# Attention and MLP block: maxima from 128 keys, weighted sums in bursts of three and four key tiles, exponentials over two PSUM banks

## The chip, the cores and the metric

The kernel runs on one core of a Trainium2 chip. The metric is the device time of one execution in microseconds. The kernel works on five engines with a queue each: PE (matmuls, with weight loads PEld), ACT (activation functions), DVE (vector operations), POOL and SP (which issues most DMAs). PE writes its results to PSUM, which has 8 banks of 128 partitions x 512 float32 values; ACT and DVE read them there.

## The reference

One transformer block over 2048 tokens of width 448, all in float32: attention with 16 query heads that share one head of keys and values (width 28), and an MLP of width 1792, both on the normalised input, added to it.

```python
xn = _layernorm(x)                      # S, D, H = 2048, 448, 16; Dh = 28
q = (xn @ wq).reshape(B, S, H, Dh)      # 16 heads of queries
k = xn @ wk                             # one head of keys and of values
v = xn @ wv
scores = einsum("bhqd,bkd->bhqk", q, k) * (Dh ** -0.5)
p = softmax(scores)
A = einsum("bhqk,bkd->bhqd", p, v) ... @ wo
h = gelu(layernorm(xn) @ w1 + b1)       # F = 1792
out = x + A + h @ w2 + b2
```

## The kernel before, in words

The first 360 us hold the projections of queries, keys and values and the MLP. Queries go to DRAM (`qd`), the MLP's result rows too (`ad`). The change lies in the rest, the attention, and in the last MLP slots that prepare it.

**Units.** Attention has `NU` = 16 units: 4 chunks of 512 queries times 4 groups of 4 heads. A unit has 16 key tiles (`kt`) of 128 keys. For each key tile and head j, PE makes a score tile of 128 keys x 512 queries (`score`, line 617, output `m`), ACT takes its exponential into `p` in SBUF (line 618), and PE multiplies it by the values into `po` (`pv`, line 791). The weighted sum of a head has 32 output columns, so four heads stand side by side in one PSUM bank; each float32 weighted sum is two matmuls in the profile, so that a key tile has 8 rows of line 791.

**Order.** Nothing reorders the instructions (`manual_schedule`): the order of the code is the order in each engine's queue. A step is two key tiles, written by `ORDERS`: `s` is a score with its exponential, `m` one job of the next unit's maxima, `n` one step of the unit's normalisation, `o` one tile of the output projection, `e` the end of the maxima, and `P` the weighted sums of `BURST` = 2 key tiles, one step behind the scores.

**PSUM in attention.** Seven single banks (`ring`, taken by `mtile` and `score`) turn around among scores, maxima and projection tiles; one bank (`op`) holds `po`. A bank is taken again when the engine that reads it has ended.

**Maxima.** The exponential needs a number per query and head near the greatest score. `max_jobs(u + 1)`, from key tile 6 of unit u on, multiplies each 128 queries by the first 256 keys (`km`, `HEAD` = 256): 16 matmuls of 256 columns in 8 jobs, each followed by one DVE reduction over a PSUM bank (line 491) into `mr`, queries on partitions. `load_max` then has PE transpose `mr` (line 472), two DVE operations negate it and split it in a high and a low part, and two DMAs write these as rows 60 and 124 of the unit's query tile `qs`, so that the score matmul subtracts them. `load_q(u)` loads a unit's queries by four DMAs; for unit 1 it is called when attention's loop begins.

**Normalisation and projection.** `norm_jobs` copies `po`, divides by the sums and splits the result (`oth`, `otl`). After the fourth unit of a chunk, `o_jobs` makes four projection tiles of 12 matmuls each (lines 686 to 688) and DVE adds them to rows loaded from `ad` (line 690). For the last chunk the parts of its first three units, nine matmuls a tile, are made within the last five steps, and those of the last unit after it, in `end_jobs`, where PE first runs idle transposes (`spin`, line 389) while DVE works.

If a sum of squares is too great, a branch (`redo`) computes attention anew with full maxima; it isn't taken here.

Of the kernel before, what the change touches and what calls it, by code (L numbers as in the profile page):

```python
# [15 lines left out]
P = 128  # L16
# [18 lines left out]
HD = D // 2  # L35
# [3 lines left out]
def block_kernel(ctx, tc, x, wq, wk, wv, wo, w1, b1, w2, b2, out):  # L39
# [4 lines left out]
    def f(t):  # L44
        return t.bitcast(F32)
# [61 lines left out]
    def mtile(shape):  # L107
        return mp.tile(shape, F32, name="m")
# [278 lines left out]
    def spin(n, t=None):  # L387
        for _ in range(n):
            pe.matmul(idle if t is None else t, ident, ident, start=True, stop=True)
# [80 lines left out]
    def spread_max(mr, qs):  # L470
        pm = mtile([4 * CT, P])
        pe.transpose(pm, mr, ident)
        mn = keep.tile([4 * CT, 2, P], F32R, name="mn", bufs=1)
        dve.tensor_scalar(mn[:, 0, :], pm, -1.0, 0.0, op0=ALU.mult, op1=ALU.add)
        dve.scalar_tensor_tensor(mn[:, 1, :], pm, -1.0, f(mn[:, 0, :]), op0=ALU.mult, op1=ALU.subtract)
        nc.sync.dma_start(f(qs[60:61, :, :]), f(mn[:, 0, :]))
        nc.sync.dma_start(f(qs[124:125, :, :]), f(mn[:, 1, :]))

    def load_max(u):
        while mxs.step():  # L480
            pass
        spread_max(mrs.pop(u), qss[u])

    def max_jobs(u):
        mrs[u] = keep.tile([P, 4 * CT], F32, name="mr", bufs=2)
        for j in range(4):
            for t in range(0, CT, 2):
                pm = mtile([P, 2, HEAD])
                for k in range(2):
                    pe.matmul(pm[:, k], qss[u][:, j, (t + k) * P:(t + k + 1) * P], km, start=True, stop=True)  # L490
                dve.tensor_reduce(mrs[u][:, CT * j + t:CT * j + t + 2], pm, axis=AX.X, op=ALU.max)  # L491
                yield

    class Stream:
        def __init__(self):
# [131 lines left out]
    for n in range(len(mslots) + LAG):  # L627
        c, ft = mslots[n] if n < len(mslots) else (NCH, n - len(mslots))
        if 3 <= ft < 11 and ft % 2 and c < NCH - 1:
            line(CT * (c + 1) + (ft - 3) // 2)  # L630
        if 9 < ft:
            line(CT * c + ft - 10)
            if ft > 10:
                a = lines[CT * c + ft - 11]
                dve.tensor_add(a, a, b2b)
        if ft == 0 and n:
            a = lines[CT * c - 1]
            dve.tensor_add(a, a, b2b)
        if (c, ft) == (NCH - 1, 7):
            load_q(0)  # L640
        if (c, ft) == (NCH - 1, 9):
            mxs.add(max_jobs(0))
        if (c, ft) == (NCH - 1, 11):
            load_max(0)
        for done, _ in enumerate(slot(n)):
            if done % 5 == 4 and (c, ft) in ((NCH - 1, 9), (NCH - 1, 10)):
# [32 lines left out]
    def o_jobs(c, gs, tiles=range(CT)):  # L679
        last = NG - 1 in gs  # L680
        for k in tiles:
            po = mtile([P, D])
            ts = slice(k * P, (k + 1) * P)
            for g in gs:
                oth, otl = ots[c, g]
                pe.matmul(po, oth[:, ts], woh[:, g, :], start=(g == gs[0]), stop=False)  # L686
                pe.matmul(po, oth[:, ts], wol[:, g, :], start=False, stop=False)  # L687
                pe.matmul(po, otl[:, ts], woh[:, g, :], start=False, stop=(g == gs[-1]))  # L688
            a = rows[c, k]
            dve.tensor_add(a, a, po)  # L690
            if last:
                (nc.scalar if k % 2 and c == NCH - 1 else nc.sync).dma_start(ov[:, CT * c + k, :], a)
            yield

    def o_tiles(c, g):
# [41 lines left out]
    def end_jobs(u, po, halves_of):  # L737
        while side.step() or oside.step():
            pass
        c, g = units[u]  # L740
        oth, otl = o_tiles(c, g)
        jobs = o_jobs(c, [g])
        tr, rb, on = att.tile([P, CW], F32, name="tr2", bufs=1), att.tile([P, CW], F32, name="tr", bufs=1), att.tile([P, CW], F32, name="oc", bufs=1)
        rc = att.tile([P, CW // 32], F32, name="rc", bufs=1)
        last = mtile([P, P])
        halves_of(1)
        sq = att.tile([P, CW], F32, name="sq", bufs=1)
        act.activation(sq, po, AF.Square, accum_out=seen[:, u:u + 1])
        spin(6, last)

        def blocks(t, h):
            return t[:, h].rearrange("p (a b) -> p a b", b=32)

        def shares(i):
            h, r = slice(256 * i, 256 * i + 256), slice(8 * i, 8 * i + 8)
            dve.transpose(tr[:, h], po[:, h])
            dve.reciprocal(rc[:, r], blocks(tr, h)[:, :, 0])
            dve.transpose(blocks(rb, h), rc[:, r, None].to_broadcast([P, 8, 32]))
            dve.tensor_mul(on[:, h], po[:, h], rb[:, h])
            act.activation(oth[:, h], on[:, h], AF.Copy)  # L760
            return lambda: dve.tensor_sub(otl[:, h], on[:, h], f(oth[:, h]))

        low = shares(0)
        low()
        low = shares(1)
        next(jobs)
        low()
        judge()
        for _ in jobs:
            pass  # L770

    pos = {}

# [12 lines left out]
    def pv(u, kt):  # L786
        if kt == 0:
            pos[u] = op.tile([P, CW], F32, name="po")
        po = pos[u]
        for j in range(4):  # L790
            pe.matmul(po[32 * j:32 * j + 32, :], vs[:, kt, :], ps.pop((u, kt, j)),  # L791
                      start=(kt == 0), stop=(kt == NT - 1))
        if kt == NT - 1:
            side.add(norm_jobs(u, pos.pop(u)))
            side.step()
            c, g = units[u]
            if c < NCH - 1 and g == NG - 1:
                oside.add(o_wait(c, range(NG), range(CT)))

    def o_wait(c, gs, tiles):  # L800
        for k in range(4):
            load_rows_of(c, tiles[k:k + 1])
            yield
            yield
        yield from o_jobs(c, gs, tiles)

    steps = [(u, kt) for u in range(NU) for kt in range(0, NT, 2)]
    pvq = [(u, kt) for u in range(NU) for kt in range(NT)]
    for n, (u, kt) in enumerate(steps):
        if n == len(steps) - 14:  # L810
            load_rows_of(NCH - 1, range(CT))
        if 4 <= n < 4 + NG:
            prep_wo(n - 4)
        if u + 1 < NU and kt == 0:
            load_q(u + 1)
        if u + 1 < NU and kt == 6:
            mxs.add(max_jobs(u + 1))
        jobs = [(u, kt + k, j) for k in range(2) for j in range(4)] if n else []
        for what in ORDERS[n % 2]:
            if what == "s" and jobs:  # L820
                score(*jobs.pop(0))
            elif what == "m":
                mxs.step()
            elif what == "e":
                if kt == 12 and u + 1 < NU:
                    load_max(u + 1)
            elif what == "n":
                side.step()
            elif what == "o":
                if n == len(steps) - 5:  # L830
                    oside.add(o_jobs(NCH - 1, range(NG - 1)))
                oside.step()
            elif what == "P":
                assert not jobs
                for _ in range(BURST if n else 0):
                    pv(*pvq.pop(0))
    assert pvq and all(u == NU - 1 for u, kt in pvq)
    pv_last(NU - 1, [kt for u, kt in pvq])
    while side.step():
        pass  # L840
    while oside.step():
# [24 lines left out]
    def general():  # L866
        for u in range(NU):
# [25 lines left out]
            dve.tensor_sub(otl, oc, f(oth))  # L893
            if g == NG - 1:
                load_rows_of(c, range(CT))
                for _ in o_jobs(c, range(NG)):
# [27 lines left out]
```

## Time and profile before

| | |
|---|---|
| median of 3 runs | 942.48 us (942.17 to 944.52) |
| the profiled execution | 944.04 us, its span 942.1 us |
| busy, share of the span | PE 98%, ACT 76%, DVE 44%, POOL 6% |
| chain that ended last | PE 90%, DVE 4%, DMA 3% |
| granted TensorE clock, mean | 0.994 |

A profile's span is the time from the first to the last instruction of one execution; its rows name the line, engine, operation, output and inputs, shape and count. In a row of groups stand busy time, mean ns of one, and the engine's idle time before them with who ended it. In a row of the timeline stand start, length, engine, line and count, and in brackets the idle time before. Matmuls overlap, so that the start of one to the start of the next is what one costs, not its length. A row of busy time by stretch has PE, PEld, DVE, ACT, POOL, then the granted clock, the DMA share and GB/s.

### The profile page before, as it was taken

How to read it: one execution, taken by the hardware profiler on the slowest of the kernel's cores; microseconds unless marked ns; L12 is line 12 of the kernel's file. 1: busy time of each engine (PE TensorE's matmuls, PEld its weight loads, DVE VectorE, ACT ScalarE, POOL GpSimd, SP SyncE). 2: the span in 40 equal slices, each digit the busy share in tenths (PEclk: the TensorE clock that was granted, in tenths of full speed). 3: DMA queues.
4: the chain of work that ended last, by engine and by line, in shares of the span. 5: the costliest groups of instructions: out<-in, count | busy, mean ns of one | idle time of the engine just before them, and what ended most of it. 6: DMA issues, size and time to landing. Idle time of an engine off the chain costs nothing.

```text
span 942.1 us, 13663 instructions
## 1 busy us (share of the span) xinstructions
PE 922.4 (98%) x5261; PEld 606.8 (64%) x5261; DVE 418.2 (44%) x812; ACT 716.2 (76%) x1366; POOL 61.1 (6%) x69
## 2 busy tenths in 40 slices
PE   9999999999999997999999999999999999999996
PEld 8778888888888875545455565455564455564554
DVE  6778776666676661233224233224232223232213
ACT  5787664554645446999999879999869999969973
POOL 4340000000000004000000000000000000000000
PEclk9999999999999999999999999999999999999999
DMA  9772212002004004101102201102201102202001
GB/s 279 223 232 79 71 47 88 21 10 88 21 10 98 0 22 113 41 1 40 41 9 52 70 31 40 41 2 59 70 31 40 41 2 59 70 30 80 1 1 42
DMA packets 34218, 54.07 MB, mean 57 GB/s; under 512 B 5207, under 2 KB 22805, under 8 KB 34149
## 3 DMA queue, kind: packets, MB, share of 16 engines
q1 hardware_dynamic: 32740, 52.58, 19.5%
q8 instruction: 42, 0.69, 0.3%
q10 hardware_dynamic: 1408, 0.57, 0.2%
q14 instruction: 28, 0.22, 0.1%
HBM read 37.40 MB, written 14.68 MB: 55 GB/s over the span
## 4 chain that ended last, share of the span: by engine, by line
PE 90%; DVE 4%; DMA 3%; ACT 1%; issue 1%; POOL 0%; SPq 0%; DVEq 0%; ACTq 0%
PE m L617 26%; PE po L791 25%; PE ph L171 12%; PE m L560 5%; PE m L557 5%; PE m L563 5%; PE m L490 4%; PE m L687 1%; PE m L686 1%; PE m L688 1%; PE ph L176 1%; PE ph L174 1%; PE qp L171 1%; PE m L263 1%; DVE xl L265 1%
## 5 line engine op out<-in xcount | busy, mean ns | idle before, releaser
L618 ACT ACTIVATE p<-m 128x512 f32<-128x512 f32 x1016 | 506.8, 643 | 61.1 <-PE m L617 59.4
L617 PE MATMUL m<-xh,ks 128*128 128x512 f32 x1024 | 282.3, 403 | 0.8 <-DVE a L567 0.8
L791 PE MATMUL po<-p,vs 128*32 128x512 f32 x2016 | 242.4, 598 | 0.0
L617 PEld LDWEIGHTS m<-xh,ks 128*128 128x128 f32 x1024 | 178.5, 189 | 83.4 <-ACT p L618 55.3
L491 DVE TENSOR_REDUCE mr<-m 128x2 f32<-128x512 f32 x128 | 88.4, 691 | 141.7 <-PE m L490 141.4
L791 PEld LDWEIGHTS po<-p,vs 128*32 128x32 f32 x2016 | 52.6, 109 | 120.8 <-issue 119.1
L531 ACT ACTIVATE hz<-ph,b1s 128x512 f32<-128x512 f32 x54 | 37.2, 688 | 112.3 <-PE ph L176 112.3
L719 DVE COPY oc<-po 128x512 f32<-128x512 f32 x15 | 10.4, 692 | 165.5 <-PE po L791 154.2
L563 PE MATMUL m<-w2h,hl 128*128 128x448 f32 x224 | 82.9, 370 | 0.0
L560 PE MATMUL m<-w2l,hh 128*128 128x448 f32 x224 | 82.0, 366 | 0.0
L557 PE MATMUL m<-w2h,hh 128*128 128x448 f32 x224 | 81.8, 365 | 0.0
L490 PEld LDWEIGHTS m<-km,xh 128*128 128x128 f32 x256 | 45.3, 191 | 49.3 <-ACT p L618 31.9
L171 PE MATMUL ph<-xh,w1h 128*128 128x512 f32 x162 | 63.9, 395 | 0.8 <-ACT hx L532 0.8
L171 PE MATMUL ph<-xl,w1h 128*128 128x512 f32 x162 | 64.0, 395 | 0.3 <-DVE xl L265 0.3
L171 PE MATMUL ph<-xh,w1l 128*128 128x512 f32 x162 | 63.9, 394 | 0.0
L490 PE MATMUL m<-km,xh 128*128 128x256 f32 x256 | 56.0, 301 | 4.3 <-DMA xh<-qd 4.3
L533 DVE TENSOR_SCALAR hz<-hz 128x512 f32<-128x512 f32 x56 | 24.6, 439 | 65.0 <-ACT hz L531 65.0
L734 POOL TENSOR_TENSOR otl<-oc,oth 128x512 fp32r<-128x512 f32 x15 | 19.3, 1289 | 502.7 <-PE m L617 281.3
L557 PEld LDWEIGHTS m<-w2h,hh 128*128 128x128 f32 x224 | 42.3, 189 | 4.8
L537 ACT ACTIVATE hz<-hz 128x512 f32<-128x512 f32 x56 | 35.2, 629 | 13.0 <-DVE hz L534 13.0
L560 PEld LDWEIGHTS m<-w2l,hh 128*128 128x128 f32 x224 | 42.1, 188 | 4.6
L563 PEld LDWEIGHTS m<-w2h,hl 128*128 128x128 f32 x224 | 42.1, 188 | 3.2
(167 smaller groups left out, 971.9 us busy)
## 6 DMA issues: line engine op xcount, KB each, us to landing
xh<-qd SPq DMA_DIRECT2D x64, 224.0 KB
a<-in_A_x_dram SPq DMA_DIRECT2D x32, 224.0 KB
qd<-qe SPq DMA_DIRECT2D x24, 256.0 KB
ad<-a SPq DMA_DIRECT2D x16, 224.0 KB
a<-ad SPq DMA_DIRECT2D x16, 224.0 KB
raw<-in_B_w_dram SPq DMA_DIRECT2D x7, 448.0 KB
out_dram<-a SPq DMA_DIRECT2D x14, 224.0 KB
raw<-in_B_w_dram SPq DMA_DIRECT2D x4, 336.0 KB
```

The costliest lines, as they stand in the source:

```text
L171: pe.matmul(ps, w, v, start=(n == 0), stop=False)
L490: pe.matmul(pm[:, k], qss[u][:, j, (t + k) * P:(t + k + 1) * P], km, start=True, stop=True)
L491: dve.tensor_reduce(mrs[u][:, CT * j + t:CT * j + t + 2], pm, axis=AX.X, op=ALU.max)
L531: act.activation(hz, ph, AF.Square, bias=b1s[:, ft:ft + 1], scale=GELU[0] ** 0.5)
L533: dve.tensor_scalar(hz, hz, 1.0, 1.0, op0=ALU.mult, op1=ALU.add)
L537: act.activation(hz, hz, AF.Tanh, scale=GELU[1])
L557: pe.matmul(m2[k], hh[:, ts], w2h[:, ft, :], start=(ft == 0), stop=False)
L560: pe.matmul(m2[k], hh[:, ts], w2l[:, ft, :], start=False, stop=False)
L563: pe.matmul(m2[k], hl[:, ts], w2h[:, ft, :], start=False, stop=(ft == NF - 1))
L617: pe.matmul(s, ks[:, kt * P:(kt + 1) * P], qss[u][:, j, :], start=True, stop=True)
L618: act.activation(p, s, AF.Exp, scale=SCALE)
L791: pe.matmul(po[32 * j:32 * j + 32, :], vs[:, kt, :], ps.pop((u, kt, j)), start=(kt == 0), stop=(kt == NT - 1))
```

## The change

Four things change together.

1. Maxima come from the first 128 keys (`HEAD` = 128). The keys are now the stationary side and 512 queries the moving one: four matmuls of 512 columns a unit, in four jobs. DVE transposes each result in 32 x 32 blocks and reduces it; `load_max` combines the four partition quarters by three DVE operations on 32 x 64, transposes, negates and splits, and four DMAs write the rows. PE transposes nothing there any more. In the MLP the first unit's four jobs lie in slots 9 and 10 as before, `load_max(0)` one slot later, and `load_q(1)` comes before attention.
2. Scores are made in pairs: two score matmuls fill a tile of two PSUM banks, and one exponential of 128 x 1024 reads it. Three such pairs (`ring`, six banks) turn around; one single bank (`single`) serves the maxima and the projection tiles of the first three chunks; `po` keeps its own.
3. Weighted sums come in bursts of 3, 3, 3, 3 and 4 key tiles (in the last unit 3, 3, 3, 3, 2, 2), each one group behind its scores; `p` has 18 pair tiles in place of 12. After each pair stand the side steps of `ORDER`.
4. The last chunk's projection: of the four parts of nine matmuls one stays before the last weighted sums, three stand in `end_jobs` in place of the idle transposes, and the parts of the last unit add to the same PSUM tiles, so that each row is added once.

```diff
-BURST = 2
-PAIRS = 12
-HEAD = 2 * P
+PAIRS = 18
+HEAD = P
-ORDERS = ("emnssmsnsmossssP", "emnssmsnsmossssP")
+ORDER = ("n", "m", "mn", "mo")
+GROUPS, LAST = (3, 3, 3, 3, 4), (3, 3, 3, 3, 2, 2)
 def load_max(u):
-        spread_max(mrs.pop(u), qss[u])
+        mb = mrs.pop(u)
+        dve.tensor_tensor(low, mb[0:32], mb[32:64], op=ALU.max)
+        dve.tensor_tensor(low, low, mb[64:96], op=ALU.max)
+        dve.tensor_tensor(low, low, mb[96:128], op=ALU.max)
+        dve.transpose(row, low)
...
+        for h, r in ((0, 60), (1, 124)):
+            for k in range(2):
+                nc.sync.dma_start(f(qss[u][r:r + 1, 2 * k:2 * k + 2, :]), f(mn[:, h, k]))
 def max_jobs(u):
         for j in range(4):
-            for t in range(0, CT, 2):
-                pm = mtile([P, 2, HEAD])
-                for k in range(2):
-                    pe.matmul(pm[:, k], qss[u][:, j, (t + k) * P:(t + k + 1) * P], km, start=True, stop=True)
-                dve.tensor_reduce(mrs[u][:, CT * j + t:CT * j + t + 2], pm, axis=AX.X, op=ALU.max)
-                yield
+            pm = mtile([P, CW])
+            pe.matmul(pm, km, qss[u][:, j, :], start=True, stop=True)
+            dve.transpose(tt, pm)
+            dve.tensor_reduce(mrs[u][:, NT * j:NT * j + NT], tt.rearrange("p (b i) -> p b i", i=32), axis=AX.X, op=ALU.max)
+            yield
-        if (c, ft) == (NCH - 1, 11):
+        if (c, ft) == (NCH - 1, 12):
             load_max(0)
+        if (c, ft) == (NCH, 0):
+            load_q(1)
-    mp = ctx.enter_context(tc.tile_pool(name="ring", bufs=7, space=PSUM))
+    mp = ctx.enter_context(tc.tile_pool(name="single", bufs=1, space=PSUM))
+    ring = ctx.enter_context(tc.tile_pool(name="ring", bufs=3, space=PSUM))
 def end_jobs(u, po, halves_of):
-        spin(6, last)
+        for k in (1, 2):
+            o_part(c, k, range(NG - 1))
...
+    def scores(u, kt, j):
+        p, s = pair_of(), ring.tile([P, 2, CW], F32, name="s")
+        for k in range(2):
+            pe.matmul(s[:, k], ks[:, kt * P:(kt + 1) * P], qss[u][:, j + k, :], start=True, stop=True)
+            ps[u, kt, j + k] = p[:, k]
+        act.activation(p, s, AF.Exp, scale=SCALE)
...
+        for size in GROUPS if u < NU - 1 else LAST:
+            group = range(at, at + size)
+            for i, (kt, j) in enumerate((kt, j) for kt in group for j in (0, 2)):
+                scores(u, kt, j)
...
+            for item in done:
+                pv(*item)
+            done = [(u, kt) for kt in group]
```

On PE before, in the second half of a middle unit, the last maxima of the next unit and the steps behind them (line 617 scores, 791 weighted sums, 490 maxima, 472 their transpose):

```order
L791 MATMUL po<-p,vs 32x512 x8
L490 MATMUL m<-km,xh 128x256 x2
L617 MATMUL m<-xh,ks 128x512 x2
L490 MATMUL m<-km,xh 128x256 x2
L617 MATMUL m<-xh,ks 128x512 x6
L791 MATMUL po<-p,vs 32x512 x8
L472 MATMUL m<-ident,mr 16x128
L617 MATMUL m<-xh,ks 128x512 x8
L791 MATMUL po<-p,vs 32x512 x8
L617 MATMUL m<-xh,ks 128x512 x8
```

The same engine after, from the last maxima of one unit to the first of the next (line 836 scores, 817 weighted sums, 501 maxima):

```order
L501 MATMUL m<-xh,km 128x512
L817 MATMUL po<-p,vs 32x512 x12
L836 MATMUL s<-xh,ks 128x512 x12
L817 MATMUL po<-p,vs 32x512 x12
L836 MATMUL s<-xh,ks 128x512 x16
L817 MATMUL po<-p,vs 32x512 x12
L836 MATMUL s<-xh,ks 128x512 x12
L817 MATMUL po<-p,vs 32x512 x16
L836 MATMUL s<-xh,ks 128x512 x12
L817 MATMUL po<-p,vs 32x512 x12
L836 MATMUL s<-xh,ks 128x512 x4
L501 MATMUL m<-xh,km 128x512
```

Turns of 8 scores and 8 weighted sums became turns of 12 or 16, and the transpose of the maxima left PE.

On DVE before, one unit's normalisation (lines 719 to 732), its eight reductions and the end of the maxima:

```order
L719 COPY oc<-po 128x512
L701 SCALAR_TENSOR_TENSOR sq,seen<-oc 128x512
L724 STREAM_TRANSPOSE tr<-oc 128x512
L726 RECIPROCAL rc<-tr 128x16
L727 STREAM_TRANSPOSE tr<-rc 128x512
L730 TENSOR_TENSOR oc<-oc,tr 128x512
L732 CAST oth<-oc 128x512
L491 TENSOR_REDUCE mr<-m 128x2 x8
L474 TENSOR_SCALAR mn<-m 16x128
L475 SCALAR_TENSOR_TENSOR mn<-m,mn 16x128
```

On DVE after, the same place behind the normalisation (`m` is the single bank, `tt` a tile in SBUF, `mr_6355` the maxima by key quarter):

```order
L503 STREAM_TRANSPOSE tt<-m 128x512
L504 TENSOR_REDUCE mr_6355<-tt 128x16
L503 STREAM_TRANSPOSE tt<-m 128x512
L504 TENSOR_REDUCE mr_6355<-tt 128x16
L484 TENSOR_TENSOR low<-mr_6355 32x64
L485 TENSOR_TENSOR low<-low,mr_6355 32x64
L486 TENSOR_TENSOR low<-low,mr_6355 32x64
L488 STREAM_TRANSPOSE row<-low 32x64
L491 TENSOR_SCALAR mb<-row 32x64
L492 SCALAR_TENSOR_TENSOR mb<-row,mb 32x64
```

Eight reductions out of PSUM became four transposes out of PSUM, each with a reduction in SBUF behind it (two of the four are shown), and six small operations stand where two stood.

More of the change, by code (lines that the diff above doesn't have):

```diff
@@ L677, in load_rows_of, with o_part, o_jobs @@
             nc.sync.dma_start(rows[c, k], ad[:, CT * c + k, :])
[L679 to L688, printed above, removed]
-            a = rows[c, k]
-            dve.tensor_add(a, a, po)
-            if last:
-                (nc.scalar if k % 2 and c == NCH - 1 else nc.sync).dma_start(ov[:, CT * c + k, :], a)
+    parts = {}
+    def o_part(c, k, gs):
+        if gs[0] == 0 and c < NCH - 1:
+            parts[c, k] = mtile([P, D])
+        elif gs[0] == 0:
+            if k % 2 == 0:
+                parts[c] = ring.tile([P, 2, CW], F32, name="s")
+            parts[c, k] = parts[c][:, k % 2, 0:D]
+        po = parts[c, k]
+        ts = slice(k * P, (k + 1) * P)
+        for g in gs:
+            oth, otl = ots[c, g]
+            pe.matmul(po, oth[:, ts], woh[:, g, :], start=(g == 0), stop=False)
+            pe.matmul(po, oth[:, ts], wol[:, g, :], start=False, stop=False)
+            pe.matmul(po, otl[:, ts], woh[:, g, :], start=False, stop=(g == NG - 1))
+        if gs[-1] == NG - 1:
+            a = rows[c, k]
+            dve.tensor_add(a, a, parts.pop((c, k)))
+            (nc.scalar if k % 2 and c == NCH - 1 else nc.sync).dma_start(ov[:, CT * c + k, :], a)
+    def o_jobs(c):
+        for k in range(CT):
+            o_part(c, k, range(NG))
             yield
@@ L761, in shares @@
             return lambda: dve.tensor_sub(otl[:, h], on[:, h], f(oth[:, h]))
-        low = shares(0)
+        shares(0)()
+        low = shares(1)
+        o_part(c, 0, [g])
+        o_part(c, 1, [g])
         low()
-        low = shares(1)
-        next(jobs)
-        low()
+        o_part(c, 3, range(NG - 1))
         judge()
-        for _ in jobs:
-            pass
+        o_part(c, 2, [g])
+        o_part(c, 3, [g])
     pos = {}
@@ L797, in pv, with o_wait, begin @@
             if c < NCH - 1 and g == NG - 1:
[L798 to L802, printed above, removed]
+                oside.add(o_wait(c))
+    def o_wait(c):
+        for k in range(CT):
+            load_rows_of(c, [k])
             yield
             yield
[L805 to L810, printed above, removed]
+        yield from o_jobs(c)
+    def scores(u, kt, j):
[4 more added lines that the diff above has]
+        act.activation(p, s, AF.Exp, scale=SCALE)
+    def begin(u, kt):
+        n = u * (NT // 2) + kt // 2
+        if n == NU * NT // 2 - 14:
             load_rows_of(NCH - 1, range(CT))
@@ L813, in block_kernel @@
             prep_wo(n - 4)
-        if u + 1 < NU and kt == 0:
+        if u and u + 1 < NU and kt == 0:
             load_q(u + 1)
@@ L817, in block_kernel @@
             mxs.add(max_jobs(u + 1))
[L818 to L838, printed above, removed]
+        if u + 1 < NU and kt == 12:
+            load_max(u + 1)
+    done = []
+    for u in range(NU):
+        at = 0
+        for size in GROUPS if u < NU - 1 else LAST:
+            group = range(at, at + size)
+            at += size
+            for i, (kt, j) in enumerate((kt, j) for kt in group for j in (0, 2)):
+                if kt % 2 == 0 and j == 0:
+                    begin(u, kt)
+                if (u, kt, j) not in ps:
+                    scores(u, kt, j)
+                for what in ORDER[2 * (kt % 2) + j // 2]:
+                    if what == "m":
+                        mxs.step()
+                    elif what == "n":
+                        side.step()
+                    elif what == "o":
+                        if (u, kt) == (NU - 1, NT - 1):
+                            o_part(NCH - 1, 0, range(NG - 1))
+                        oside.step()
+            for item in done:
+                pv(*item)
+            done = [(u, kt) for kt in group]
+    pv_last(NU - 1, [kt for u, kt in done])
     while side.step():
@@ L895, in general @@
                 load_rows_of(c, range(CT))
-                for _ in o_jobs(c, range(NG)):
+                for _ in o_jobs(c):
                     pass
```

13 lines of the change are left out of this document (9 added, 4 removed).

## The prediction

> **What bounds the kernel now.** I read the page's groups first, then the busy time of the attention stage, its timeline, and last single rows of that timeline for the gaps. The groups (mean ns of one, then idle time and who ended it) say how large each stream is:
> ```profile
> span 942.1 us, 13663 instructions
> L618 ACT ACTIVATE p<-m 128x512 f32<-128x512 f32 x1016 | 506.8, 643 | 61.1 <-PE m L617 59.4
> L617 PE MATMUL m<-xh,ks 128*128 128x512 f32 x1024 | 282.3, 403 | 0.8 <-DVE a L567 0.8
> L791 PE MATMUL po<-p,vs 128*32 128x512 f32 x2016 | 242.4, 598 | 0.0
> 360.10:928.50 568.40, 564.13 (x3515) 298.31 (x3515) 162.59 (x302) 506.84 (x1016) 28.66 (x25) 1.00 0.15 39
> ```
> The last row is the attention stage: PE busy 564.1 of 568.4 us, ACT 506.8. So PE is the bound, ACT follows at 89%, DVE (162.6) has room. The steady rhythm, with one row per burst:
> ```profile
> 663.93 1.92 PE L791 MATMUL po<-p,vs 128*32 128x512 f32 x16
> 665.78 2.11 PE L617 MATMUL m<-xh,ks 128*128 128x512 f32 x8
> 667.82 1.93 PE L791 MATMUL po<-p,vs 128*32 128x512 f32 x16
> 658.33 14.00 ACT L618 ACTIVATE p<-m 128x512 f32<-128x512 f32 x28 [0.59 <-PE m L617]
> 651.02 1.92 PE L791 MATMUL po<-p,vs 128*32 128x512 f32 x16
> 655.64 1.92 PE L791 MATMUL po<-p,vs 128*32 128x512 f32 x16
> 660.02 1.92 PE L791 MATMUL po<-p,vs 128*32 128x512 f32 x16
> ```
> A step of two key tiles is 1.85 of weighted sums (663.93 to 665.78) and 2.04 of scores (to 667.82): 3.89. ACT does 28 exponentials in 14.00, 0.50 each, 8 per step 4.0: PE and ACT are almost level, and ACT never stops because seven PSUM banks lie between them. Steps with maxima are 0.73, 0.49 longer (651.02 to 655.64, to 660.02): 0.24 per pair of 256-wide matmuls, 1.95 per unit (3+3+2 pairs).
>
> The gaps, from single rows:
> ```profile
> 663.61 0.39 PE L617 MATMUL m<-xh,ks 128*128 128x512 f32 x1
> 664.38 1.47 PE L791 MATMUL po<-p,vs 128*32 128x512 f32 x12
> 665.24 0.61 PE L791 MATMUL po<-p,vs 128*32 128x512 f32 x4
> 665.78 0.50 PE L617 MATMUL m<-xh,ks 128*128 128x512 f32 x1
> 666.12 0.40 PE L617 MATMUL m<-xh,ks 128*128 128x512 f32 x1
> 666.32 0.61 ACT L618 ACTIVATE p<-m 128x512 f32<-128x512 f32 x1
> 663.39 1.59 ACT L618 ACTIVATE p<-m 128x512 f32<-128x512 f32 x3
> 664.34 1.61 ACT L618 ACTIVATE p<-m 128x512 f32<-128x512 f32 x3
> ```
> PE: second score 0.34 after the first, last score to burst 0.32 (663.61 to 663.93), so the six gaps between are 0.23 each; weighted sums come in waves of four 0.45, then 0.43 apart; the last wave to the next score 0.54. Three tiles are 2.71, four 3.57. ACT starts 0.04 after the score ended (666.28); back to back, two take 0.95 (663.39 to 664.34), 0.475 each.
>
> **The change, part by part.**
>
> *Exponential over two banks.* Not in the trace. Nearest rows:
> ```profile
> L537 ACT ACTIVATE hz<-hz 128x512 f32<-128x512 f32 x56 | 35.2, 629 | 13.0 <-DVE hz L534 13.0
> L333 ACT ACTIVATE w2h<-raw 128x896 fp32r<-128x896 f32 x7 | 6.6, 944 | 0.0
> L618 ACT ACTIVATE first<-m 128x512 f32<-128x512 f32 x8 | 4.7, 595 | 2.4 <-PE m L617 2.3
> ```
> 384 more elements cost 0.315, so 512 more cost 0.42. Alone: 0.595 + 0.42 = 1.02. Back to back: 0.475 + 0.42 = 0.90. Bounds: 0.84 (1024 elements and nothing else) and 1.00 (two singles at 0.50); I take 0.90, the row's own slope. Each pair saves ACT 0.05 to 0.1, 25 to 50 us over 512 pairs, but of an engine that isn't the bound.
>
> The Trainium skill, "Perfetto Trace Analysis", section "Optimizing Scalar/DVE Operations", says that larger operations raise throughput if the engine is saturated, but that where an unsaturated ACT causes bubbles on others, breaking instructions up lets work finish sooner. By its first half the stage would shrink by those 25 us or more, to about 915; by its second the time would rise, and ACT's 89% above puts this kernel there.
>
> *What stands between PE and ACT.* Seven single banks become three pairs, a pair being free only when its whole exponential has ended. A pair here is the two 512-wide scores that one exponential reads. What waits on PE is a score; behind it in PE's queue stand the rest of the group and then its burst, so a late bank delays everything, and nobody else can use PE meanwhile. I follow one group (three key tiles, six pairs), from its first score, all pairs free:
> - pair 1: second score 0.34, ended 0.74, exponential 0.78 to 1.80; the next end 0.90 apart: 2.70, 3.60, 4.50...
> - pairs 2 and 3 go out unhindered; pair 4 would start at 1.50 but waits for 1.80 + 0.04; pair 5 for 2.74, pair 6 for 3.64.
> - pair 6's second score 3.98, burst 4.30 (unhindered: 0.34 + 10 x 0.23 + 0.32 = 2.96).
> - burst of three 2.71: next group at 7.01.
>
> The same time read from ACT: six exponentials are 5.4 of the 7.01. When the burst begins ACT has at most the rest of three pairs, about 2.1; new scores reach it 2.71 + 0.78 later, so it stands idle for 1.4 in every group. Before, the burst was 1.85 and seven banks held 3.5 of work. Two tiles a step took 3.89, three 5.84 at that rate; a group takes 7.01. With four tiles scored it takes 8.81, with four summed 7.87. A unit: 3 x 7.01 + 7.87 + 8.81 = 37.7.
>
> *Maxima.* Eight pairs of 256-wide matmuls become four 512-wide ones, cost 0.92 in place of 1.95, but each uses the one single bank, which a DVE transpose frees and which its reduce delays for the next:
> ```profile
> L724 DVE STREAM_TRANSPOSE tr<-oc 128x512 f32<-128x512 f32 x15 | 10.6, 706 | 0.0
> L491 DVE TENSOR_REDUCE mr<-m 128x2 f32<-128x512 f32 x128 | 88.4, 691 | 141.7 <-PE m L490 141.4
> ```
> DVE takes them 0.71 + 0.69 = 1.40 apart, while PE asks for the bank after every pair or two, with the group's remaining scores queued behind it. First transpose at 1.47, third ends 4.98, the fourth matmul at 5.02, burst at 5.34 instead of 4.30: 1.0 per unit on the path (bounds 0, if hidden, and 1.95). Unit: 38.7. The six small DVE operations and the four row stores (two before) of the tail come at key tile 12, some 9 us before their unit: nothing waits for them; the engine with room covers them.
>
> *A unit before*, from the transposed maxima of units 1 and 15, and nine projection matmuls:
> ```profile
> 387.11 0.28 PE L472 MATMUL m<-ident,mr 128*16 128x128 f32 x1
> 880.04 0.28 PE L472 MATMUL m<-ident,mr 128*16 128x128 f32 x1
> 906.10 0.19 PEld L686 LDWEIGHTS m<-woh,oth 128*128 128x128 f32 x1
> 907.96 0.85 PEld L617 LDWEIGHTS m<-xh,ks 128*128 128x128 f32 x4
> ```
> 492.93 for 14 units less 12 projection tiles at 12/9 x 1.86 = 2.48: 33.1 each. Middle units: 14 x (38.7 - 33.1) = +78.4. In the new order a projection tile fills waiting time, about 0.35 each (0 to 0.7): -4.
>
> *Start, load_q(1) earlier, no PE transpose of maxima.*
> ```profile
> PE m L490 <- DMA xh<-qd: 4.3, 1, 4.3
> PE m L472 <- DVE mr L491: 2.0, 1, 2.0
> 334.00:342.00 8.00, 8.00 (x31) 6.71 (x30) 3.52 (x8) 2.42 (x4) 0.00 (x0) 0.79 0.21 62
> 350.00:400.00 50.00, 44.94 (x259) 26.75 (x258) 12.19 (x21) 38.01 (x76) 10.05 (x10) 0.97 0.28 72
> ```
> These single waits go, and the granted clock behind each (0.79 of 8 us, 0.97 of 50) gives back 1.7 and 1.5. Before attention: -2.0 - 1.7, and -1.0 for the first unit's maxima. Unit 0: before 7 x 3.89 + 1.95 + 5.8 = 35.0; after, its first eight pairs 6.1 + 2.71, then 8.0 + 7.0 + 8.8: 32.6, so -2.4. The load's POOL memset and four DMAs move ahead of attention on SP; behind them only stores and the output weights queue, which have until unit 3.
>
> *Last unit and end.* Groups 3, 3, 3, 3, 2, 2 give 7.87 + 3 x 7.01 + 5.2 + 4.4 = 38.5, with one part of nine matmuls 40.4; before 8 x 3.89 + 4 x 1.86 = 38.6: +1.8. The other three parts run in the end, where PE spins and waits:
> ```profile
> 928.52 1.60 PE L389 MATMUL m<-ident 128*128 128x128 f32 x12
> 931.54 0.47 PE L686 MATMUL m<-woh,oth 128*128 128x448 f32 x1 [1.42 <-ACT oth L760]
> 938.15 0.62 DVE L690 TENSOR_TENSOR a<-a,m 128x448 f32<-128x448 f32 x1 [0.50 <-PE m L688]
> ```
> Two parts (3.7) cover 928.5 to 931.5 and 0.7 more; the third hides in the wait for the second half; I take -1.5 (-4 to +2).
>
> **Sum.** 78.4 - 4 - 4.7 - 2.4 + 1.8 - 1.5 = +67.6 on the span of 942.1: 1009.7. The runs' median is 0.4 above that span (the profiled run itself took 944.04): 1010.
>
> **Rivals.**
> A, faster: PE stays the bound since three pairs are enough. A mode change costs PE the long gaps 0.54, 0.32 and 0.34, and there are 5 bursts per unit in place of 8. Unit 4 x 2.96 + 3.91 + 4 x 2.71 + 3.57 + 0.92 = 31.1 against 33.1; with start and end about 895. It decides if pair 4's bank is free at 1.50, an exponential of 0.68 for 1024 elements; 0.595 for 512 speaks against it. The Trainium skill, "TensorEngine Tiling (Array Packing)", "Key Properties", says a change of tiling mode drains the engine, which is this rival's rule; the trace's 0.54 agrees. Chance 0.05.
> B, slower still: the waits inside a group halve the granted clock, as the single waits of 2.0 and 4.3 did. The new waits are at most 0.6 each, with matmuls between; a tenth of the stage at half clock adds some 25: 1035. Chance 0.06.
> C, level: start, end and cheaper maxima outweigh a milder starvation, 942; that needs a group at 5.9 instead of 7.01, below the 6.8 that 0.84 per pair gives. Chance 0.02.
>
> **Numbers.** Forecast, starvation of ACT by three pairs: 0.87. Its range: 0.84 per pair (-17), hidden maxima (-15), second scores at 0.23 after a wait (-9) below; 1.00 per pair (+20) and rival B above. Not all together: 985 to 1032. Slower by over 0.3%, about what a measurement here tells from no change, 0.93; within 0.02; faster 0.05.
>
> **What would show it.** ACT rows of 128x1024 at a mean near 1.0, busy near 465 in a stage of 635 to 640; PE idle "<-ACT p" at the score line, in two or three places of each group; ACT idle over 1 us before each group's first pair; a group of 12 scores and 24 sum rows every 7.0; the single waits at the start gone. Wrong it is if a score never waits for ACT, or if groups come every 5.7.

## The result and the profile after

The changed kernel takes 1031.52 us (median of 4 runs, 1030.59 to 1032.41); the kernel before, 942.94 (4 runs, 942.17 to 944.52). The ratio is 1.0937 with an interval of 1.0918 to 1.0956: slower by 9.4%. The forecast of 1010 had the direction and the mechanism, and the time lies at the upper edge of its range of 985 to 1032.

The first lines of the page after: the span, then busy time, share of the span and instructions of each engine, then the chain that ended last by engine.

```profile
span 1028.6 us, 13314 instructions
PE 954.0 (93%) x5041; PEld 572.8 (56%) x5041; DVE 429.5 (42%) x872; ACT 685.7 (67%) x858; POOL 61.0 (6%) x69
PE 74%; ACT 13%; DVE 8%; issue 3%; DMA 1%; ACTq 0%; DVEq 0%; POOL 0%; SPq 0%; POOLq 0%
```

PE fell from 98% of the span to 93%, ACT from 76% to 67%, and ACT has 13% of the last chain, which before named PE, DVE and DMA first: neither engine is full now, they wait for each other in turn. The groups of the same page (busy, mean ns of one | idle time before them and who ended it):

```profile
L838 ACT ACTIVATE p<-s 128x1024 f32<-128x1024 f32 x508 | 476.4, 1042 | 178.4 <-PE s L836 178.4
L836 PE MATMUL s<-xh,ks 128*128 128x512 f32 x1016 | 322.1, 425 | 43.5 <-ACT p L838 42.7
L817 PE MATMUL po<-p,vs 128*32 128x512 f32 x2016 | 232.8, 596 | 0.0
L501 PE MATMUL m<-xh,km 128*128 128x512 f32 x64 | 29.8, 466 | 15.3 <-DVE tt L503 13.9
```

The exponentials need 30 us less in all (476.4 for 506.8), which is what the wide instruction was to give. But ACT now stands idle for 178 us waiting for scores (61 before), PE waits 42.7 us for exponentials where the row of the scores before (L617, in the prediction) has no idle time put down to ACT, and 13.9 us for the one bank of the maxima. The attention stage as one stretch (PE, PEld, DVE, ACT, POOL, clock, DMA share, GB/s):

```profile
354.12:1011.68 657.56, 596.28 (x3293) 264.36 (x3293) 171.97 (x358) 476.36 (x508) 26.92 (x24) 1.00 0.12 32
```

It is 657.6 us long against 568.4, at a full granted clock. The rhythm, from the timeline of PE and ACT (start, length, engine, line, count, idle time before):

```profile
649.16 1.20 PE L836 MATMUL s<-xh,ks 128*128 128x512 f32 x4
651.39 0.50 PE L501 MATMUL m<-xh,km 128*128 128x512 f32 x1 [0.34 <-DVE tt L503]
652.94 0.51 PE L501 MATMUL m<-xh,km 128*128 128x512 f32 x1 [0.58 <-DVE tt L503]
654.48 0.50 PE L501 MATMUL m<-xh,km 128*128 128x512 f32 x1
654.91 2.78 PE L817 MATMUL po<-p,vs 128*32 128x512 f32 x24
657.62 1.65 PE L836 MATMUL s<-xh,ks 128*128 128x512 f32 x6
658.45 5.61 ACT L838 ACTIVATE p<-s 128x1024 f32<-128x1024 f32 x6 [2.52 <-PE s L836]
659.53 0.73 PE L836 MATMUL s<-xh,ks 128*128 128x512 f32 x2 [0.26 <-ACT p L838]
660.45 0.73 PE L836 MATMUL s<-xh,ks 128*128 128x512 f32 x2 [0.18 <-ACT p L838]
661.36 0.73 PE L836 MATMUL s<-xh,ks 128*128 128x512 f32 x2 [0.18 <-ACT p L838]
662.03 2.78 PE L817 MATMUL po<-p,vs 128*32 128x512 f32 x24
664.74 1.66 PE L836 MATMUL s<-xh,ks 128*128 128x512 f32 x6
665.57 2.86 ACT L838 ACTIVATE p<-s 128x1024 f32<-128x1024 f32 x3 [1.51 <-PE s L836]
```

Read it as the prediction's group. Three pairs of scores go out at once from 657.62 (the row of 6). The fourth has no bank until the first exponential, which began at 658.45, has ended; it starts at 659.53, the next two at 660.45 and 661.36, 0.92 and 0.91 later, which is ACT's pace. Only then, at 662.03, can the burst begin. During it ACT works off the pairs that are left and then stands for 1.51 us (the bracket of 665.57). A group takes 7.12 us (657.62 to 664.74); three key tiles took 5.84 before. With the maxima (first four rows) it takes longer still: 649.16 to 657.62 is 8.46, since a maxima matmul can't start until DVE has emptied the one bank, 1.55 after the last (651.39, 652.94, 654.48).

### The profile page after: what moved, and what is told of

It is laid out like the page before. It is cut to its first block, busy times and chain, and to the rows that moved or that the text cites. A ratio compares the mean times of both kernels' runs of the same rounds, so it can differ in the third digit from the quotient of the medians.

```text
span 1028.6 us, 13314 instructions
## 1 busy us (share of the span) xinstructions
PE 954.0 (93%) x5041; PEld 572.8 (56%) x5041; DVE 429.5 (42%) x872; ACT 685.7 (67%) x858; POOL 61.0 (6%) x69
## 4 chain that ended last, share of the span: by engine, by line
PE 74%; ACT 13%; DVE 8%; issue 3%; DMA 1%; ACTq 0%; DVEq 0%; POOL 0%; SPq 0%; POOLq 0%
PE po L817 22%; PE s L836 17%; ACT p L838 12%; PE ph L171 11%; PE m L573 4%; PE m L570 4%; PE m L576 4%; DVE tt L503 3%; DVE mr L504 2%; PE qp L171 1%; PE ph L176 1%; PE ph L174 1%; PE m L501 1%; PE m L708 1%; PE m L709 1%
## 5 line engine op out<-in xcount | busy, mean ns | idle before, releaser
L838 ACT ACTIVATE p<-s 128x1024 f32<-128x1024 f32 x508 | 476.4, 1042 | 178.4 <-PE s L836 178.4
L836 PE MATMUL s<-xh,ks 128*128 128x512 f32 x1016 | 322.1, 425 | 43.5 <-ACT p L838 42.7
L836 PEld LDWEIGHTS s<-xh,ks 128*128 128x128 f32 x1016 | 168.1, 188 | 219.3 <-ACT p L838 172.8
L817 PE MATMUL po<-p,vs 128*32 128x512 f32 x2016 | 232.8, 596 | 0.0
L817 PEld LDWEIGHTS po<-p,vs 128*32 128x32 f32 x2016 | 57.4, 109 | 130.3 <-issue 126.3
L503 DVE STREAM_TRANSPOSE tt<-m 128x512 f32<-128x512 f32 x64 | 45.8, 716 | 72.4 <-PE m L501 67.9
L760 POOL TENSOR_TENSOR otl<-oc,oth 128x512 fp32r<-128x512 f32 x15 | 19.3, 1287 | 595.0 <-DVE oth L758 396.5
L550 ACT ACTIVATE hz<-hz 128x512 f32<-128x512 f32 x56 | 35.2, 629 | 15.1 <-DVE hz L547 15.1
L504 DVE TENSOR_REDUCE mr<-tt 128x16 f32<-128x512 f32 x64 | 43.9, 686 | 2.2
L501 PE MATMUL m<-xh,km 128*128 128x512 f32 x64 | 29.8, 466 | 15.3 <-DVE tt L503 13.9
```

The costliest lines, as they stand in the source:

```text
L501: pe.matmul(pm, km, qss[u][:, j, :], start=True, stop=True)
L503: dve.transpose(tt, pm)
L504: dve.tensor_reduce(mrs[u][:, NT * j:NT * j + NT], tt.rearrange("p (b i) -> p b i", i=32), axis=AX.X, op=ALU.max)
L550: act.activation(hz, hz, AF.Tanh, scale=GELU[1])
L836: pe.matmul(s[:, k], ks[:, kt * P:(kt + 1) * P], qss[u][:, j + k, :], start=True, stop=True)
L838: act.activation(p, s, AF.Exp, scale=SCALE)
```

## The experiments

Each is the changed kernel with the edit shown, unless said otherwise. Comparisons are with the kernel before on the same chip; experiments 1 to 4 have two runs each, 5 to 7 four. Differences from the changed kernel, and between experiments, are between times taken on more than one occasion, for which the kernel before had medians of 942.2 to 943.8 us, so that a microsecond or two of such a difference means nothing.

**1. Two pairs instead of three.** If the number of pairs is what ACT starves on, one fewer must make each group longer by about an exponential.

```diff
-    ring = ctx.enter_context(tc.tile_pool(name="ring", bufs=3, space=PSUM))
+    ring = ctx.enter_context(tc.tile_pool(name="ring", bufs=2, space=PSUM))
```

> Two PSUM pairs in place of three, all else as changed. Starvation theory: the third pair of a group now waits where the fourth did, and two exponentials of 0.915 us more lie between it and the group's sixth pair's bank, less the one that the third pair's own wait replaces: each group is one exponential (0.915 us) longer, 80 groups, +65 to +75 us, about 1100 us; the groups of three come every 8.03 us in place of 7.12. Rival (the exponential over two banks is itself the limit, ACT bound): ACT has the same work, so the time stays within 10 us of 1031.

Measured: 1097.45 us, ratio 1.1631 (1.1592 to 1.167), 66 above the changed kernel. PE's timeline of this run:

```profile
615.00 2.78 PE L817 MATMUL po<-p,vs 128*32 128x512 f32 x24
617.72 1.20 PE L836 MATMUL s<-xh,ks 128*128 128x512 f32 x4
619.62 0.74 PE L836 MATMUL s<-xh,ks 128*128 128x512 f32 x2 [0.71 <-ACT p L838]
```

Four scores go out at once instead of six and the wait before the next is 0.71. The next burst of this run begins at 623.11: a group of 8.11, 1.0 more than with three pairs. The 66 is at the low end of the 65 to 75 expected: four of a unit's five groups grow by about 1.0, while the group with maxima stays at 8.46 (632.08 to 640.54). What was found for three pairs holds for two.

**2. Bursts of two key tiles, pairs kept.** If starvation rules, shorter bursts make it milder; if the price is the change of mode on PE (rival A's term), eight bursts in place of five make it worse.

```diff
-GROUPS, LAST = (3, 3, 3, 3, 4), (3, 3, 3, 3, 2, 2)
+GROUPS, LAST = (2,) * 8, (2,) * 8
```

> Three pairs as changed, but weighted sums in bursts of two key tiles. Starvation theory: with four pairs a group only the fourth waits (at 1.91 us), the burst is 1.85 in place of 2.71, so a group of two takes 4.43 us against 7.12 for three: 2.22 us per key tile against 2.37; about -2 to -3 us per unit, the maxima's waits staying: 985 to 1000 us. Rival (switches between scores and weighted sums are what costs, fewer bursts are better): three more bursts per unit at some 0.34 us each, 16 units: +16 us, about 1047.

Measured: 998.73 us, ratio 1.0585 (1.0531 to 1.0639), 33 us less than the changed kernel. PE's timeline of this run:

```profile
605.22 1.92 PE L817 MATMUL po<-p,vs 128*32 128x512 f32 x16
607.07 1.67 PE L836 MATMUL s<-xh,ks 128*128 128x512 f32 x6
608.99 0.73 PE L836 MATMUL s<-xh,ks 128*128 128x512 f32 x2 [0.24 <-ACT p L838]
609.65 1.93 PE L817 MATMUL po<-p,vs 128*32 128x512 f32 x16
```

Now one pair of four waits, where three of six did. Two key tiles take 4.43 (605.22 to 609.65) against 4.74 in the changed kernel (two thirds of 7.11) and 3.89 before. More changes of mode, less time: rival A's price isn't what decides here.

**3. The maxima spread out.** Two of four side steps hold a maxima job instead of three, so that the single bank is asked for less often.

```diff
-ORDER = ("n", "m", "mn", "mo")
+ORDER = ("n", "m", "n", "mo")
```

> One job of the maxima per key tile in place of three per two, all else as changed: four jobs now lie two pairs (1.83 us) apart, more than the 1.55 us that transpose and reduction take on DVE. If the 1.35 us by which the group with maxima is longer (8.46 against 7.11) is the wait for the single bank: 10 to 20 us less, 1011 to 1021. If it is the matmuls and DVE work themselves: no change within 4 us.

Measured: 1016.43 us, ratio 1.0773 (1.0738 to 1.0808), 15.1 us less. PE's timeline of this run, two groups that hold maxima:

```profile
639.46 2.78 PE L817 MATMUL po<-p,vs 128*32 128x512 f32 x24
643.22 0.39 PE L501 MATMUL m<-xh,km 128*128 128x512 f32 x1
644.65 0.40 PE L501 MATMUL m<-xh,km 128*128 128x512 f32 x1
646.82 2.78 PE L817 MATMUL po<-p,vs 128*32 128x512 f32 x24
653.93 2.78 PE L817 MATMUL po<-p,vs 128*32 128x512 f32 x24
```

These groups take 7.36 and 7.11, so that a unit's maxima cost 0.25 in place of 1.35; the matmuls no longer have a wait in brackets. Over 14 middle units that is 15.4, about the whole of the gain. The maxima matmuls are almost free between scores that wait anyway; it was the wait for the one bank that cost.

**4. Six single banks in place of three pairs.** Bursts stay; the pairing goes, in the scores and in the last chunk's four projection parts, which get a bank each. An exponential of one bank frees it after 0.48 instead of 0.92, but ACT does twice as many.

```diff
-    ring = ctx.enter_context(tc.tile_pool(name="ring", bufs=3, space=PSUM))
+    ring = ctx.enter_context(tc.tile_pool(name="ring", bufs=6, space=PSUM))
...
-            if k % 2 == 0:
-                parts[c] = ring.tile([P, 2, CW], F32, name="s")
-            parts[c, k] = parts[c][:, k % 2, 0:D]
+            parts[c, k] = ring.tile([P, CW], F32, name="s")[:, 0:D]
...
-        p, s = pair_of(), ring.tile([P, 2, CW], F32, name="s")
+        p = pair_of()
         for k in range(2):
-            pe.matmul(s[:, k], ks[...], qss[u][:, j + k, :], start=True, stop=True)
+            s = ring.tile([P, CW], F32, name="s")
+            pe.matmul(s, ks[...], qss[u][:, j + k, :], start=True, stop=True)
+            act.activation(p[:, k], s, AF.Exp, scale=SCALE)
-        act.activation(p, s, AF.Exp, scale=SCALE)
```

> The same six banks as single tiles with an exponential of 512 each, bursts of 3, 3, 3, 3, 4 as changed; the last chunk's four parts get a bank each. Starvation theory: a bank comes back after 0.6 us in place of 1.05 and a score follows at once, so the seventh score waits less: stage about 25 us shorter although ACT does 508 instructions more (0.98 per two against 0.915): 1000 to 1012 us. Rival (an exponential of two banks saves ACT time and that is what counts): 508 x 0.065 = 33 us longer, about 1064.

Measured: 1010.77 us, ratio 1.0713 (1.0676 to 1.0749), 20.7 us less. PE's timeline of this run, and its end as one stretch:

```profile
609.40 2.78 PE L815 MATMUL po<-p,vs 128*32 128x512 f32 x24
612.11 4.14 PE L835 MATMUL s<-xh,ks 128*128 128x512 f32 x12
616.17 2.78 PE L815 MATMUL po<-p,vs 128*32 128x512 f32 x24
995.54:1009.20 13.66, 8.48 (x45) 7.24 (x41) 6.38 (x17) 1.52 (x4) 0.00 (x0) 0.94 0.20 72
```

The group takes 6.77 instead of 7.11. With the same six banks the pairing alone costs 0.34 in a group of three, though ACT is quicker with it. The row of the twelve scores has no wait in brackets, since matmuls overlap; that they wait shows in their 4.06 (612.11 to 616.17), where twelve without a wait take 2.96 by the prediction's gaps. The group with maxima, held by its single bank, stays at 8.46 (600.94 to 609.40). So the attention is 16.1 us shorter (641.4 for 657.6), and the other 3.3 on the span come from the end, 13.7 for 16.9, which has nothing to do with the exponentials. The expected 1000 to 1012 held, near its top.

**5. No pairs and no bursts.** Seven single banks that scores, maxima and projection tiles share, exponentials per bank, bursts of two. What is left of the change is the maxima from 128 keys, the earlier `load_q(1)` and the re-ordered end.

```diff
-GROUPS, LAST = (3, 3, 3, 3, 4), (3, 3, 3, 3, 2, 2)
+GROUPS, LAST = (2,) * 8, (2,) * 8
-    mp = ctx.enter_context(tc.tile_pool(name="single", bufs=1, space=PSUM))
-    ring = ctx.enter_context(tc.tile_pool(name="ring", bufs=3, space=PSUM))
+    mp = ctx.enter_context(tc.tile_pool(name="ring", bufs=7, space=PSUM))
...
-        p, s = pair_of(), ring.tile([P, 2, CW], F32, name="s")
+        p = pair_of()
         for k in range(2):
...
+            s = mtile([P, CW])
...
+            act.activation(p[:, k], s, AF.Exp, scale=SCALE)
...
-        act.activation(p, s, AF.Exp, scale=SCALE)
```

> The changed kernel with seven single banks shared by scores, maxima and projection, an exponential per bank, and bursts of two: what is left of the change is the maxima from 128 keys, the earlier load and the end. Starvation theory: no group waits any more; a unit is 8 x 3.89 + 0.92 = 32.0 us against 33.1, so -16 us for the units, -6 before attention and -6 for unit 0's wait, -6 for the parts moved to the end and +2 there: 905 to 920 us, faster than both. Rival (the new maxima, on DVE and in row stores, are part of what slowed the kernel): not under 942.

Measured: **918.98 us**, ratio 0.9752 (0.9735 to 0.9768): faster than both kernels. Of this run the span, PE's timeline (the steps with maxima first, then plain ones) and the two stretches of attention and end:

```profile
span 917.9 us, 13361 instructions
598.40 1.92 PE L812 MATMUL po<-p,vs 128*32 128x512 f32 x16
603.43 1.92 PE L812 MATMUL po<-p,vs 128*32 128x512 f32 x16
607.58 1.92 PE L812 MATMUL po<-p,vs 128*32 128x512 f32 x16
644.08 1.92 PE L812 MATMUL po<-p,vs 128*32 128x512 f32 x16
648.00 1.92 PE L812 MATMUL po<-p,vs 128*32 128x512 f32 x16
354.10:903.23 549.13, 548.33 (x3294) 273.90 (x3293) 172.50 (x360) 501.76 (x1016) 27.75 (x24) 1.00 0.15 39
903.23:917.90 14.67, 8.48 (x45) 7.24 (x41) 6.38 (x17) 1.53 (x4) 0.00 (x0) 0.88 0.20 68
```

The plain step is 3.92 (644.08 to 648.00; the next one 3.90), that of the kernel before, and PE is busy for 548.3 of the 549.1 us of attention. So the parts that are left are worth 24 on the span of 942.1: 19.3 in attention (549.1 for 568.4), 6.0 ahead of it (354.1 for 360.1), less 1.1 at the end (14.7 for 13.6).

The expectation had 28 in the attention (16 for the units, 6 for unit 0's wait, 6 for the parts moved to the end), and what fell short are the maxima. The two steps that hold them take 5.03 and 4.15 (598.40, 603.43, 607.58), together 1.37 more than two plain ones, where 0.92 was assumed; a middle unit takes 32.6 for 33.1, so that they save 0.5 a unit in place of 1.0, some 8 us in all. Unit 0 is 5.5 shorter up to its key tile 12 (its wait of 4.3 is gone), and the three parts that moved to the end took 1.8 each: together that is 19 of the 19.3. These shares are read from the rows; they weren't run apart.

**6. Bursts alone.** The kernel of experiment 5 with the changed kernel's bursts.

```diff
-GROUPS, LAST = (2,) * 8, (2,) * 8
+GROUPS, LAST = (3, 3, 3, 3, 4), (3, 3, 3, 3, 2, 2)
```

> As the kernel without pairs and bursts, but bursts of 3, 3, 3, 3, 4. Starvation theory: a group's last scores still wait, the twelfth for the fifth exponential (0.54 + 0.60 + 4 x 0.49 = 3.10, against 2.64), so three tiles take 6.2 us in place of 5.84 and four scored 8.1: +25 to +30 us against that kernel, 935 to 947. Rival (only the two-bank release starves ACT; longer bursts save switches): 890 to 905, below that kernel.

Measured: 955.76 us, ratio 1.0142 (1.0125 to 1.0159): 36.8 above experiment 5, where at most 30 was expected. PE's and ACT's timeline of this run:

```profile
646.46 3.65 PE L832 MATMUL m<-xh,ks 128*128 128x512 f32 x12
647.00 5.99 ACT L833 ACTIVATE p<-m 128x512 f32<-128x512 f32 x12 [1.17 <-PE m L832]
650.04 2.78 PE L812 MATMUL po<-p,vs 128*32 128x512 f32 x24
652.75 1.19 PE L832 MATMUL m<-xh,ks 128*128 128x512 f32 x4
653.29 5.99 ACT L833 ACTIVATE p<-m 128x512 f32<-128x512 f32 x12 [0.30 <-PE m L832]
657.30 2.78 PE L812 MATMUL po<-p,vs 128*32 128x512 f32 x24
```

Even seven banks don't cover these bursts: ACT stands for 0.30 after a burst of three (the bracket of 653.29) and for 1.17 after one of four (647.00; the burst before it, from 642.89, is of four): 0.87 more for 0.86 more of burst. A group of three takes 6.29 (646.46 to 652.75), 0.1 more than expected, and ACT's twelve exponentials fill 5.99 of it.

The groups were expected nearly right; the expectation's sum was not. Its 6.2 and 8.1, with 7.1 for the group of four summed that it left out, add up to 33.8 a unit without maxima (3 x 6.2 + 8.1 + 7.1), and eight steps of 3.89 to 31.1: 2.6 more a unit, some 40 in 15 units, where it said 25 to 30. Measured, a unit takes 35.2 with its maxima (7.26, 6.28, 8.25, 6.28 and 7.14) against 32.6 in experiment 5, which is 2.6 again. The maxima themselves add no more here than there: their group's scores and maxima run from 652.75 to 657.30, 4.55 for 3.58 in a group without, 0.97 against 1.37.

**7. The end's projection in banks of its own.** In the changed kernel two projection parts of the end lie in the two halves of one PSUM pair. Here each has its own.

```diff
-            if k % 2 == 0:
-                parts[c] = ring.tile([P, 2, CW], F32, name="s")
-            parts[c, k] = parts[c][:, k % 2, 0:D]
+            parts[c, k] = ring.tile([P, 2, CW], F32, name="s")[:, 0, 0:D]
```

> The changed kernel, but each of the last chunk's four parts gets a PSUM pair of its own, where two shared one. If PE's waits of 1.07 and 0.71 us at the end are for DVE's addition out of the other half of the same pair: -2 to -4 us, about 1028. If the end waits for the shares themselves: within 1 us of 1031.

Measured: 1030.78 us (1028.16 to 1032.55), ratio 1.093 (1.0911 to 1.095): not told apart from the changed kernel by the time. The end alone, a stretch of the changed kernel first:

```profile
1011.68:1028.60 16.92, 9.01 (x45) 7.09 (x41) 6.48 (x17) 1.52 (x4) 0.00 (x0) 0.84 0.16 58
```

and of this run:

```profile
1015.70:1030.50 14.80, 8.75 (x45) 7.17 (x41) 6.38 (x17) 1.52 (x4) 0.00 (x0) 0.87 0.19 66
562.00:580.00 18.00, 16.03 (x86) 9.11 (x85) 6.86 (x10) 6.78 (x8) 0.86 (x1) 0.91 0.07 26
```

The end is shorter by 2.1, as expected; but attention ended 4.0 later, which the edit doesn't touch. The second stretch shows one place of it: a granted clock of 0.91 over 18 us. PE's timeline there, a projection tile:

```profile
571.49 0.47 PE L706 MATMUL m<-woh,oth 128*128 128x448 f32 x1 [1.04 <-DVE tt L503]
573.25 0.57 PE L707 MATMUL m<-wol,oth 128*128 128x448 f32 x1
573.62 0.57 PE L708 MATMUL m<-woh,otl 128*128 128x448 f32 x1
```

Matmuls come 0.37 apart instead of 0.20: about half the clock, for 3.4 us, in two places of this run (573 and 740), which at half speed lose some 3.4 of the 4.0. They follow three waits for the single bank in a row (0.35, 0.58 and 1.04 within 4 us). In the changed kernel's profile the same three waits stand without a drop (a clock of 1.00 from 562 to 576), while 10 us with a mean clock of 0.83 stand in experiments 1 (from 956) and 4 (from 560) too. So whether the drop comes differs between executions, and the 2.1 of the end is within that scatter.

**Together.** With the new maxima and the re-ordered end in all four, in us:

| | bursts of 2 | bursts of 3 and 4 |
|---|---|---|
| seven single banks, shared | 919.0 | 955.8 |
| three pairs and one single bank | 998.7 | 1031.5 |

Bursts cost 37 alone and 33 on top of pairs; pairs with their single bank cost 80 alone. The two costs nearly add up, and the rest of the change gains 24.

## Why the prediction was right, and where its numbers were off

**The bound.** Right: starvation of ACT by three pairs. The marks it named stand in the trace: a mean of 1042 ns for 128x1024, waits for ACT before three pairs of a group, ACT idle for 1.51 before a group, groups of 7.1, and the single waits at the start gone. Two came larger than it said: ACT's exponentials are busy for 476 us (near 465), in a stage of 658 (635 to 640). Experiment 1 (fewer pairs) and 2 (shorter bursts) moved the time the way and by the amount that this mechanism gives, and experiment 5, without it, is faster than before. That 1031.5 still lies within 985 to 1032, by half a microsecond, is in part luck: the upper end was drawn for exponentials of 1.00 a pair and for half clock; the first came to 0.915, the second not at all in the changed kernel's attention, and what filled the range instead are terms below that the prediction had too small.

**The group.** 7.11 for 7.01; with four scored 8.94 for 8.81; with four summed 7.98 for 7.87. The whole chain of steps held, each a little too short: fourth pair 1.91 after the first score (1.84), pairs 0.915 apart (0.90), burst at 4.41 (4.30), burst 2.71 as said. The exponential back to back was 0.915 (5.61 for six, 1.04 for one) where the slope of other rows gave 0.90. That is about 0.55 a unit, 8 us over 14.

**The maxima.** Mis-sized: 1.35 a unit instead of 1.0. The transpose and the reduction were taken as 1.40 apart; with the gaps between them it is 1.55, four jobs a unit. Experiment 3 showed the price directly: 15.1 us for the waits on this bank. That is 5 us beyond the estimate. The 0.92 taken for the four matmuls themselves is no fixed price either: with seven shared banks they cost 1.37 a unit (experiment 5).

**The middle units.** From the two terms above a unit is 39.6 (7.11 + 8.94 + 7.11 + 7.98 + 8.46) in place of 38.7: 12.6 of the 18.9 us by which the span (1028.6) exceeds the forecast's 1009.7. Start and end below add 3.5. Of the other 2.8 some 1.1 are the projection tiles, which cost 2.23 each where 2.13 was forecast (four tiles add 8.90 to the three groups from 550.38 to 582.83); the rest lies in the first and last unit and wasn't separated.

**Before attention.** -6.0 for -4.7. The wait for the maxima is gone, as in unit 0 the wait for the load, and the granted clock stays at 1.00 through the attention.

**The end.** The sign failed: 16.9 us from the end of the attention instead of 13.6 before, +3.3 for -1.5. The step that failed: the prediction put three parts into waiting time, and overlooked that two parts share a PSUM pair, so that a matmul into one half waits for DVE's addition out of the other. PE's and DVE's rows of the changed kernel:

```profile
1017.27 0.47 PE L708 MATMUL s<-woh,oth 128*128 128x448 f32 x1 [1.07 <-DVE a L713]
1018.18 0.62 DVE L713 TENSOR_TENSOR a<-a,s 128x448 f32<-128x448 f32 x1 [0.97 <-PE s L710]
1021.60 0.47 PE L708 MATMUL s<-woh,oth 128*128 128x448 f32 x1 [0.71 <-DVE a L713]
```

Experiment 7 gave back 2.1 of the 4.8: its two waits of 1.07 and 0.71 became one of 0.45, where four parts ask for three pairs. In experiment 4, where each part has a bank of its own, PE has no such wait and the end takes 13.7, 3.3 less. So the shared pair is worth 2 to 3 us, and even without it the end is no shorter than before: the forecast gain of 1.5 came in no run, and its cause stays open.

**Span and time.** The prediction put the time 0.4 above the span, by setting the median of the runs (942.48) against the span of an execution that itself took 944.04. In the runs here the time is 1.8 to 2.1 above that run's own span, some 1.6 us more; and the profiled execution of the changed kernel is the fastest of its four, 0.9 below their median.

**The rivals.** A fell: more changes of mode made the kernel faster (experiment 2 and experiment 5 against 6), so what a change costs, the 0.54 and 0.32 of the rows, isn't what decides here. The Trainium skill's "TensorEngine Tiling (Array Packing)", section "Key Properties", has the rule that a change of tiling mode drains the engine; the gaps of 0.54 and 0.32 agree with it. C fell with the time. B, half clock, was there in a small form in experiment 7's run; in the changed kernel's profile the attention ran at 1.00. The rule of the Trainium skill that spoke against the change, "Perfetto Trace Analysis", section "Optimizing Scalar/DVE Operations" (where Scalar or Vector isn't saturated but causes bubbles on other engines, breaking up instructions may let work end sooner), agrees with experiment 4: the same six banks with broken-up exponentials save 0.34 in a group of three.

**Where the gain of the wide exponential went.** ACT's 30 us came off an engine that wasn't the bound. The price of a bank can be read across the runs: a group of three takes 8.11 with two pairs and 7.11 with three; 6.77 with six singles and 6.29 with seven. A pair more buys 1.0, a single bank more 0.48, in both cases about one exponential of that size (0.915 and 0.475).

## What to carry to other kernels

As far as these runs go, the work that a PSUM ring holds, counted in the reading engine's time, must outlast the longest stretch in which the writing engine does something else, plus its restart: here three pairs of 0.92, of which hardly more than two still hold work when the burst begins, stood against 2.71 + 0.83. A wider instruction on the reading engine saves that engine time but hands buffers back later, which is a loss where it isn't the bound; and a bank set aside for one kind of job makes its jobs queue at the full pace of whoever empties it. Of a change with several parts, run the cheap parts alone: here they were worth 2.5%, hidden under a loss of 112 us.

## What the runs showed that was not expected

- The maxima from 128 keys save 0.5 us a unit when they share seven banks with the scores, half of what their four matmuls at 0.23 each would give.
- No row before showed an exponential over two PSUM banks. It takes 1.04 us on average and 0.915 to the next one, when pairs follow each other, near the 1.02 and 0.90 that were worked out; one of a single bank takes 0.475 to 0.50. The second bank adds 0.42 to 0.44.
- The granted clock fell to half for 3.4 us after three waits of 0.35, 0.58 and 1.04 us within 4 us, in one execution and not in another with the same waits.
